# ScalarE takes the weights' low bits and batch 0's sums of squares, with a new order of work in the first stretch

## The chip, the cores and the metric

The kernel runs on one core of a Trainium2 chip. The metric is the device time of one execution in microseconds. The engines are TensorE (PE in the profile), VectorE (DVE), ScalarE (ACT), GpSimd (POOL) and SyncE (SP). SP, POOL and ACT also issue DMA transfers.

## The reference

Per batch (8) and head (8) there are 512 local and 32 global tokens of width 64. Global queries look at all keys; local queries look at the 32 global keys and at the local keys within 32 positions. The two outputs, in one tensor of 4608 x 512, go through a two-layer block: `h = x @ w_in` (512 x 2048), `g = h * tanh(log1p(exp(h)))`, `out = g @ w_out` (2048 x 512), in float32 at the end.

`w_in` and `w_out` come as float64, since a float32 array is scaled there by a float64 number. All else is float32. So the kernel sees each weight as two 32-bit words, and makes its float32 out of them with integer operations: bits 31 and 30 of the high word stay, its low 27 bits go up by three, and the top three bits of the low word come in below.

## The kernel before

**Tiling.** Attention goes by batch, pair of heads (hp, four of them) and query tile of 128 rows (t, four of them): scores (L895), row minimum with the mask (L921 on VectorE), exponential (L930 on ScalarE), a split of the result into two float16 parts, a transpose, and the product with V's two float16 parts (L1020). V's parts need a power of two as their scale, from the largest absolute value of the batch: `b_max` and `b_scale`, where POOL reduces over the partitions. For batch 0 the first two query tiles are transposed on TensorE (`p_cross`, L971 and L985; `x_cross`, L996 and L1004), which copies out of PSUM to `pt`, `xh` and `xl`.

The dense part goes by blocks of 256 tokens, 17 in all, and by eight slices of the inner dimension. The first product is `m1_mm` (L1173) and later `st_mm` (L1342); the second is `m2_mm` (L1437) and at the end `ms_mm` (L1532). Each float32 operand is again two float16 parts, three matmuls per product.

**Weights.** 32 blocks k of 128 x 512 float64 numbers, 0 to 15 of `w_in` and 16 to 31 of `w_out`, are loaded by `w_load` (512 KB each): 0 to 4 from ACT's queue, the others from POOL's. A load waits until its buffer is free. Per block VectorE runs `w_bits` (L630: shift and mask of the high word) and the two operations of `w_sum` (L637: the top two bits; L639: the low word, shifted). Then `w_stat` (L660) sums squares of the block on TensorE, and after the sixteenth block `w_norm` makes the scale from it: VectorE reduces (L671), POOL reduces over the partitions (L676), VectorE finishes. Only then `w_split` can write the float16 parts: the high ones on ScalarE (L537) or VectorE, the low ones on VectorE (L715), for the first four slices on TensorE (L709, L710) with a copy (L530). Loads 21 and up also wait for the reduction L671.

**Order.** [...] `Plan` gathers all tasks with their dependences, plays them against a table of costs and gives each engine a list. Then `MOVES` takes single tasks out of these lists: `231 P 196` puts task 231 right after task 196 on TensorE (P; V is VectorE, A ScalarE, G POOL, S the queue of SP). Tasks that may run on either engine change it in this way too. Each engine works through its list in order, and a waiting instruction holds up what is behind it.

Task numbers count the calls of `add`, so both versions number alike. Those that the prediction names:

- 196, 231: scores of batch 0, pair 0 and pair 1. 202, 211, 243: V's low parts of pairs 0 and 1, and the copy of pair 2's out of PSUM.
- 23: the identity times V's scale. 210, 250: V's high parts of pairs 1 and 3.
- 226, 288, 331: the copies of a `p_cross` out of PSUM (two instructions of 256 columns each); 304, 306, 337: those of an `x_cross` (one each).
- 342: a copy for `w_split` 1; 360, 382, 464: high parts of `w_split` 3, 4 and 7 (1024 columns). 402, 430, 479: high parts of probabilities. 462: an output of the global queries.
- 244, 253: the first small copy of V's rows for pairs 2 and 3, on SP's queue. 338: the load of batch 1's V, also there.

`VMAX` picks the batches whose V scale comes from squares on ScalarE; at 99 it picks none.

Of the kernel before, what the change touches and what calls it, by code (L numbers as in the profile page):

```python
# [73 lines left out]

MOVES = [(int(n), e, int(m)) for n, e, m in (x.split() for x in """91 P 271, 92 P 91, 93 P 92, 307 P 95, 284 P 275, 154 P 313, 350 P 154, 318 P 159, 164 P 330, 169 P 422, 174 P 343, 175 P 348, 176 P 358, 177 P 378, 178 P 392, 389 P 397, 398 P 389,
461 P 398, 179 P 421, 180 P 453, 454 P 180, 181 P 454, 450 P 474, 182 P 450, 475 P 182, 510 P 475, 183 P 510, 185 P 468, 557 P 555, 513 P 556, 526 P 558, 573 P 565, 566 P 573, 559
P 594, 664 P 642, 562 P 664, 580 P 562, 665 P 580, 680 P 665, 681 P 680, 703 P 622, 704 P 703, 625 P 629, 645 P 634, 666 P 645, 672 P 651, 652 P 672, 673 P 669, 705 P 673, 745 P
684, 747 P 745, 715 P 690, 716 P 708, 731 P 746, 732 P 748, 757 P 754, 769 P 757, 758 P 769, 818 P 783, 808 P 800, 35 V 18, 36 V 19, 37 V 20, 38 V 22, 232 V 39, 233 V 46, 43 V 233,
47 V 43, 44 V 47, 261 V 50, 262 V 54, 58 V 262, 56 V 62, 282 V 67, 283 V 71, 291 V 283, 296 V 291, 76 V 296, 267 V 81, 72 V 267, 73 V 83, 78 V 87, 292 V 88, 115 V 292, 111 V 115,
112 V 268, 274 V 297, 107 V 327, 101 V 107, 108 V 309, 103 V 322, 298 V 103, 104 V 298, 113 V 104, 380 V 113, 116 V 380, 328 V 116, 117 V 351, 123 V 119, 352 V 329, 127 V 366, 131  # L80
V 127, 373 V 424, 132 V 425, 133 V 135, 129 V 133, 374 V 129, 439 V 374, 381 V 136, 407 V 139, 137 V 407, 387 V 137, 403 V 387, 388 V 144, 370 V 388, 151 V 370, 371 V 151, 413 V
371, 372 V 413, 414 V 372, 418 V 414, 408 V 418, 384 V 408, 385 V 145, 148 V 448, 156 V 383, 157 V 431, 161 V 157, 412 V 161, 419 V 158, 449 V 419, 471 V 449, 149 V 471, 420 V 149,
396 V 466, 434 V 166, 459 V 401, 446 V 459, 163 V 171, 467 V 163, 168 V 172, 429 V 173, 472 V 429, 465 V 472, 529 V 465, 186 V 529, 480 V 186, 511 V 480, 534 V 188, 483 V 189, 457
V 483, 522 V 191, 512 V 478, 193 V 512, 524 V 193, 540 V 524, 535 V 540, 525 V 489, 195 V 525, 444 V 195, 906 V 444, 530 V 906, 536 V 531, 220 V 536, 907 V 220, 908 V 545, 230 V
908, 542 V 230, 260 V 550, 552 V 260, 520 V 560, 583 V 520, 584 V 583, 278 V 561, 910 V 578, 958 V 579, 587 V 585, 590 V 587, 591 V 588, 959 V 648, 649 V 959, 639 V 569, 620 V 639,
960 V 620, 961 V 960, 554 V 961, 786 V 554, 962 V 610, 624 V 962, 1001 V 643, 1002 V 644, 1003 V 1002, 575 V 1003, 1004 V 575, 687 V 1004, 1005 V 687, 1035 V 657, 621 V 1035, 1208
V 658, 688 V 1208, 1036 V 688, 667 V 678, 650 V 667, 631 V 650, 1037 V 631, 632 V 1037, 1209 V 632, 661 V 1209, 636 V 661, 668 V 636, 784 V 682, 637 V 683, 696 V 785, 697 V 810,
728 V 697, 729 V 706, 812 V 729, 654 V 707, 655 V 723, 700 V 655, 675 V 700, 813 V 1039, 676 V 813, 737 V 1062, 815 V 772, 738 V 815, 850 V 773, 1063 V 850, 730 V 1063, 693 V 1064,
694 V 752, 741 V 694, 718 V 741, 719 V 753, 1066 V 767, 768 V 1066, 776 V 1123, 821 V 776, 805 V 1124, 822 V 805, 806 V 1125, 779 V 734, 760 V 735, 761 V 790, 744 V 816, 1127 V
744, 1146 V 1127, 826 V 817, 1147 V 826, 823 V 1147, 787 V 823, 834 V 787, 797 V 834, 1148 V 797, 798 V 876, 802 V 798, 837 V 802, 803 V 864, 844 V 843, 235 A 226, 294 A 286, 295 A  # L90
294, 105 A 304, 317 A 105, 316 A 314, 312 A 316, 325 A 312, 335 A 331, 326 A 335, 355 A 340, 369 A 337, 342 A 438, 345 A 342, 440 A 344, 402 A 440, 360 A 347, 357 A 360, 359 A 349,
416 A 377, 379 A 416, 417 A 382, 451 A 417, 445 A 399, 395 A 445, 400 A 433, 462 A 400, 458 A 462, 427 A 458, 452 A 427, 469 A 452, 428 A 479, 463 A 428, 470 A 464, 477 A 456, 521
A 477, 482 A 521, 518 A 190, 192 A 443, 538 A 192, 539 A 538, 514 A 194, 219 A 514, 515 A 219, 527 A 515, 541 A 544, 528 A 229, 570 A 528, 519 A 259, 551 A 519, 277 A 551, 909 A
563, 279 A 564, 581 A 279, 567 A 582, 568 A 567, 711 A 609, 646 A 626, 656 A 627, 677 A 647, 713 A 677, 630 A 713, 635 A 630, 1038 A 660, 695 A 685, 720 A 686, 849 A 762, 692 A
849, 717 A 692, 740 A 717, 775 A 770, 804 A 771, 733 A 804, 836 A 833, 481 S 436, 523 S 485, 543 S 547, 640 S 593, 712 S 640, 659 S 749, 679 S 659, 714 S 679, 739 S 702, 764 S 739,
807 S 777""".split(","))]
# [1862 lines left out]
```

## Time and profile before

| | |
|---|---|
| median of 3 runs | 873.93 us (872.58 to 873.93) |
| the profiled execution | 873.65 us, of which the span is 871.9 |
| mean granted TensorE clock | 0.995 |
| DMA | 111.07 MB, mean 127 GB/s |

The span reaches from the first to the last instruction; 1.75 us of the execution lie around it. The page gives busy times over the whole span. The stages differ much, so the table of windows is the one to read first: each of its lines gives a stretch, its length, each engine's busy time in it with the number of instructions, the granted clock as a share of full speed, the mean busy share of the DMA engines, and GB/s. A busy engine is not always at its peak: the ends of matmuls are modelled.

### The profile page before, as it was taken

To read this page: it belongs to the slowest core of one execution; us is meant where nothing else is said; L and a number is where in the kernel's file an instruction comes from. 1 tells how busy PE (TensorE), PEld (TensorE's weight loads), DVE (VectorE), ACT (ScalarE), POOL (GpSimd) and SP (SyncE) were. 2 spreads that over 40 slices of the span, in tenths; PEclk is the share of its full clock that TensorE was granted. 3 is DMA by queue.
4 is the path that set the end of the run, shared out by engine and by line. 5 is a ranking of instruction groups with operands and counts; after the bars stand their busy time and mean duration, and the time that the engine had idled before them with its cause. 6 is when DMAs were issued, how large, how long until landed. Compare 5 with 4: busy or idle time off the path is not lost.

```text
span 871.9 us, 24740 instructions
## 1 busy us (share of the span) xinstructions
PE 840.7 (96%) x9792; PEld 620.8 (71%) x9792; DVE 747.9 (86%) x1989; ACT 645.9 (74%) x1389; POOL 169.4 (19%) x324
## 2 busy tenths in 40 slices
...
GB/s 365 372 358 92 120 153 115 60 145 101 180 216 124 194 136 131 150 107 183 126 121 104 170 131 101 89 165 121 122 116 118 89 77 38 1 27 14 14 27 25
DMA packets 206885, 111.07 MB, mean 127 GB/s; under 512 B 186992, under 2 KB 191280, under 8 KB 205744
## 3 DMA queue, kind: packets, MB, share of 16 engines
...
q10 hardware_dynamic: 864, 2.88, 0.9%
...
## 4 chain that ended last, share of the span: by engine, by line
PE 89%; DVE 6%; DMA 2%; ACT 1%; issue 0%; POOL 0%; DVEq 0%; ACTq 0%
PE o L1437 33%; PE h L1342 25%; PE h L1173 11%; PE s L895 5%; PE U L1020 5%; PE o L1532 5%; PE gu L1124 1%; PE g L1058 1%; DVE W L637 1%; DMA raw<-in_w 1%; DVE W L639 1%; DVE W L630 1%; DMA W<-in_w 1%; DMA pt<-ph 1%; PE hx L1532 1%; DVE vmx L744 1%
## 5 line engine op out<-in xcount | busy, mean ns | idle before, releaser
L1437 PE MATMUL o<-W,G 128*128 128x512 f16 x1344 | 313.2, 379 | 0.0
L1437 PEld LDWEIGHTS <-G 128*128 128x128 f16 x1344 | 124.9, 98 | 128.5 <-issue 2.6
L1342 PEld LDWEIGHTS <-W 128*128 128x128 f16 x2880 | 166.0, 98 | 9.6 <-issue 0.2
L930 ACT ACTIVATE P<-P,nm 128x192 f32<-128x192 f32 (+1 forms) x256 | 117.8, 461 | 38.8 <-DVE nm L921 38.2
L1173 PE MATMUL h<-xh,W 128*128 128x256 f16 x640 | 114.4, 273 | 0.0
L1173 PEld LDWEIGHTS <-W 128*128 128x128 f16 x960 | 91.1, 98 | 16.7 <-issue 3.0
L1342 PE MATMUL h<-xh,W 128*128 128x128 f16 x1056 | 97.0, 219 | 0.0
L1342 PE MATMUL h<-xl,W 128*128 128x128 f16 x528 | 91.1, 219 | 0.0
L1173 PE MATMUL h<-xl,W 128*128 128x256 f16 x320 | 87.2, 272 | 0.0
L1342 PE MATMUL h<-raw,W 128*128 128x128 f16 x1152 | 73.2, 219 | 0.0
L854 POOL DMA_DIRECT2D vc<-vf x81 | 41.3, 512 | 155.6 <-DVE vf L835 110.3
L1020 PEld LDWEIGHTS <-pt 128*128 128x128 f16 (+1 forms) x1424 | 56.1, 98 | 18.9 <-issue 7.7
L895 PE MATMUL s<-qk 64*128 64x224 f16 (+3 forms) x640 | 56.2, 301 | 7.3 <-DMA qk<-in_qk 6.4
L921 DVE CUSTOM_DVE_ANT_0 P<-s,consts,sq 128x192 f32<-128x192 f32 (+1 forms) x128 | 53.0, 429 | 10.3 <-PE s L895 10.3
L537 ACT ACTIVATE ph<-P 128x384 f16<-128x384 f32 (+1 forms) x112 | 58.7, 538 | 3.3 <-DMA pt<-ph 2.6
L854 POOL DMA_DIRECT2D vgg<-vgf x84 | 44.3, 531 | 85.0 <-issue 47.9
L921 DVE CUSTOM_DVE_ANT_0 P<-s,consts 128x192 f32<-128x192 f32 (+1 forms) x128 | 45.5, 369 | 9.0 <-PE s L895 4.4
L1020 PE MATMUL U<-vc,pt 96*128 96x64 f16 (+1 forms) x656 | 52.3, 193 | 0.0
L1020 PE MATMUL U<-vf,pt 128*128 128x64 f16 x720 | 50.7, 194 | 0.7 <-DMA pt<-ph 0.7
L930 ACT ACTIVATION_READ_ACCUMULATOR P<-P,nm 128x1 f32 x256 | 48.1, 188 | 0.0
L530 ACT COPY EE<-h 128x512 f32<-128x512 f32 x47 | 27.2, 579 | 23.4 <-PE h L1342 16.2
L949 DVE SCALAR_TENSOR_TENSOR ph<-P,ph 128x256 f16<-128x256 f32 x112 | 38.5, 353 | 4.1 <-ACT ph L537 3.5
(281 smaller groups left out, 1750.8 us busy)
## 6 DMA issues: line engine op xcount, KB each, us to landing
...
W<-in_w POOLq DMA_DIRECT2D x14, 512.0 KB, 7.5
raw<-in_w POOLq DMA_DIRECT2D x7, 512.0 KB, 7.3
G<-in_w POOLq DMA_DIRECT2D x6, 512.0 KB, 6.8
W<-in_w ACTq DMA_DIRECT2D x5, 512.0 KB, 10.6
pt<-ph SPq DMA_TRANSPOSE x120, 3.6
```

Of the source, the lines that this page charges most:

```text
L530: A.copy(dst, src)
L537: A.activation(out=dst, in_=src, func=AF.Copy, scale=c)
L854: stream(POOL, dma(kib), lambda: G.dma_start(dst(), src()), 512, r=[r], w=[w], new=new, table="dma")
L895: T.matmul(X[s[h]][:, cols(u)], part(b, hp, i)[r, u * 128:(u + 1) * 128], part(b, hp, j)[r, KO + OWN[u]:KO + OWN[u] + WIDTH[u]], start=n = ...
L921: pl.add(DVE, (134 if b >= QF else 77) + 1.03 * w, lambda: V.tensor_tensor_reduce(out=half(P, h, w), in0=X[s][:, cols(t)], in1=mask[:, m0: ...
L930: pl.add(ACT, 460, lambda: A.activation(out=half(P, h, w), in_=half(P, h, w), func=AF.Exp, bias=X[nm], scale=-1.0, accum_out=X[sums][:, t, ...
L949: pl.add(DVE, dve(2 * (z - a)), lambda a=a, z=z, q=q, o=o: V.scalar_tensor_tensor(X[ph][:, q, :, a + o:z + o], p_src(X[P], t)[:, :, a:z], ...
L1020: T.matmul(X[u][:, t, h, :], X[pt][:k, p * 4 + (c * 2 + h if turned(b, t) else h * 2 + c), :], X[vx][:k, t, vl, h * 64:(h + 1) * 64], star ...
L1173: T.matmul(X[h][:, f * TB:(f + 1) * TB], wh(i, wl)[:, off:off + 128], X[x][:, d, o:o + TB], start=(n == 0), stop=(n == 11))
L1342: T.matmul(X[h][:, c:c + 128], form(J + jj, wl)[:, off:off + 128], x(l, d), start=(p in (1, 2, 5) and c == 0 and n == 0), stop=(n == 5), s ...
L1437: T.matmul(X[o], gp(g, blk, i)[:, f, t * 128:(t + 1) * 128], wh(8 + i, wl)[:, f * 512:(f + 1) * 512], start=(turn == 0 and n == 0), stop=( ...
L1532: T.matmul(X[o][:, cols], a_form(a, jj, f), b_form(w, jj, f), start=(fresh and n == 0), stop=(n == 11), skip_group_check=True)
```

## The change

For each weight block, the second operation of `w_sum` on VectorE becomes a task of ScalarE: `w_low` reads the upper 16 bits of the low word, and by scale, bias and rounding to bfloat16 leaves their top three bits as the low bits of a bfloat16 number, which it writes over the lower half of the high word. The remaining VectorE operation, `w_join`, takes the top two and the low three bits of that word in one. `w_low` comes after `w_bits`, which still reads the whole high word, and `w_join` after `w_low`.

For batch 0 the V scale comes from the largest sum of squares of a partition, over 512 numbers (128 for the global rows), on ScalarE, instead of the largest absolute value on VectorE. `MOVES` is another list, of 413 entries instead of 344: 75 for TensorE (60 before), 213 for VectorE (199), 101 for ScalarE (74), 21 for SP (11) and 3 for POOL (none). Its highest task number stays the same. The diff is cut in the two lists; of the new one, the lines stand here that hold the entries named above.

```diff
@@ -14,6 +14,7 @@
 I32 = mybir.dt.int32
 U32 = mybir.dt.uint32
 BF16 = mybir.dt.bfloat16
+U16 = mybir.dt.uint16
 AF = mybir.ActivationFunctionType
 ALU = mybir.AluOpType
 AX = mybir.AxisListType
@@ -66,34 +67,39 @@
 STACKED = 1
 PELOW = 4
 STAT = 2
-VMAX = 99
+VSQ = (0,)
+BY_ACT = range(32)
 
 
 PE, DVE, ACT, POOL, DMA = "PE", "DVE", "ACT", "POOL", "DMA"
 
 
-MOVES = [(int(n), e, int(m)) for n, e, m in (x.split() for x in """91 P 271, 92 P 91, 93 P 92, 307 P 95, 284 P 275, 154 P 313, 350 P 154, 318 P 159, 164 P 330, 169 P 422, 174 P 343, 175 P 348, 176 P 358, 177 P 378, 178 P 392, 389 P 397, 398 P 389,
...
+MOVES = [(int(n), e, int(m)) for n, e, m in (x.split() for x in """231 P 196, 202 P 231, 211 P 202, 225 P 74, 237 P 225, 227 P 237, 242 P 84, 281 P 242, 239 P 281, 251 P 90, 269 P 91, 271 P 95, 234 P 97, 263 P 234, 100 P 287, 307 P 275, 284 P 299,
...
+745 P 684, 747 P 745, 715 P 690, 691 P 715, 716 P 708, 751 P 725, 746 P 751, 748 P 731, 818 P 783, 31 V 29, 35 V 31, 32 V 35, 20 V 198, 13 V 221, 37 V 13, 22 V 37, 34 V 22, 23 V
+34, 25 V 23, 38 V 222, 210 V 38, 232 V 210, 40 V 42, 46 V 40, 226 V 48, 50 V 261, 250 V 50, 266 V 262, 52 V 266, 243 V 54, 62 V 56, 283 V 58, 66 V 283, 71 V 60, 64 V 71, 68 V 292,
+78 V 68, 86 V 73, 296 V 86, 267 V 83, 297 V 267, 268 V 88, 274 V 107, 288 V 274, 308 V 109, 111 V 308, 327 V 309, 298 V 322, 104 V 115, 304 V 104, 328 V 119, 323 V 328, 351 V 323,
+306 V 351, 352 V 306, 121 V 352, 380 V 121, 405 V 123, 406 V 329, 331 V 406, 365 V 331, 384 V 125, 366 V 384, 423 V 127, 131 V 423, 424 V 131, 337 V 424, 425 V 337, 129 V 425, 370
+V 129, 135 V 370, 139 V 135, 371 V 139, 342 V 371, 439 V 342, 381 V 439, 373 V 381, 402 V 133, 374 V 402, 360 V 374, 387 V 360, 441 V 387, 388 V 441, 413 V 388, 137 V 413, 414 V
+137, 372 V 414, 403 V 372, 385 V 147, 382 V 156, 448 V 382, 383 V 448, 151 V 383, 407 V 166, 430 V 407, 149 V 431, 412 V 149, 419 V 412, 471 V 419, 396 V 471, 420 V 466, 459 V 420,
+171 V 459, 446 V 171, 434 V 446, 472 V 434, 408 V 168, 401 V 408, 464 V 401, 429 V 464, 529 V 429, 462 V 529, 465 V 173, 479 V 534, 480 V 535, 511 V 480, 457 V 511, 473 V 457, 512
...
+1147 V 826, 823 V 1147, 787 V 823, 834 V 787, 797 V 834, 1148 V 797, 798 V 876, 802 V 798, 837 V 802, 199 A 36, 200 A 199, 33 A 200, 223 A 201, 14 A 223, 224 A 39, 43 A 224, 47 A
...
+248, 338 S 253, 481 S 436, 596 S 481, 484 S 596, 485 S 484, 597 S 523, 750 S 597, 546 S 750, 547 S 546, 572 S 543, 592 S 589, 593 S 592, 712 S 640, 714 S 679, 662 S 714, 663 S 662,
...
@@ -634,6 +640,17 @@
         if not w64:
             return
         f, key = lambda: wf(k).bitcast(I32), wkeys(k)
+        if k in BY_ACT:
+
+            def w_low():
+                halves = raw(k).bitcast(U16).rearrange("p (f w) -> p f w", w=4)
+                A.activation(out=halves[:, :, 2].bitcast(BF16), in_=halves[:, :, 1], func=AF.Copy, scale=2.0 ** -8, bias=4336 + 2.0 ** -9)
+            pl.add(ACT, act(512), w_low, r=key, w=[rawkey(k)])
+
+            def w_join():
+                V.scalar_tensor_tensor(f(), word(k, 1), -0x3FFFFFF9, f(), ALU.bitwise_and, ALU.bitwise_or)
+            pl.add(DVE, 610, w_join, r=[rawkey(k)], w=key)
+            return
         pl.add(DVE, 610, lambda: V.scalar_tensor_tensor(f(), word(k, 1), -0x40000000, f(), ALU.bitwise_and, ALU.bitwise_or),
                r=[rawkey(k)], w=key)
         pl.add(DVE, 610, lambda: V.scalar_tensor_tensor(f(), word(k, 0), 29, f(), ALU.logical_shift_right, ALU.bitwise_or),
@@ -731,7 +748,7 @@
 
     def b_max(b, hp):
         m = ("vmx", b)
-        if b >= VMAX:
+        if b in VSQ:
             src = lambda: X["vraw", b][:, hp].rearrange("p a c -> p (a c)") if hp < HP else X["vgraw", b]
             n = 512 if hp < HP else 128
             pl.add(ACT, act(n) + 90, lambda: A.activation(out=junk[:, :n] if b > 1 else X["vj", b][:, :n], in_=src(), func=AF.Square, accum_out=X[m][:, hp:hp + 1]),
@@ -756,7 +773,7 @@
 
         def go():
             q, s = X[p], X[sv]
-            if b >= VMAX:
+            if b in VSQ:
                 V.tensor_scalar(q, q, TINY * TINY, None, ALU.max)
                 V.tensor_scalar(q.bitcast(I32), q.bitcast(I32), 1, 0x7F800000, ALU.logical_shift_right, ALU.bitwise_and)
                 V.tensor_scalar(q, q, 2.0 ** 63, None, ALU.mult)
@@ -1874,7 +1891,10 @@
         pl.settle()
 
     V.memset(pmax, 0.0)
-    pl.add(POOL, 600, lambda: G.partition_all_reduce(warm, pmax, 128, RED.max))
+
+    def warm_up():
+        G.partition_all_reduce(warm, pmax, 128, RED.max)
+    pl.add(POOL, 600, warm_up)
     for i, x in enumerate(ORDER.split()):
         a, n = x[0], int(x[1:] or 0)
         pl.slot = LOAD1 + LOADS1 * i
```

## Rows read from the trace of the kernel before

**Rows 1.** The page: busy time of each engine over the whole span.
```profile
PE 840.7 (96%) x9792; PEld 620.8 (71%) x9792; DVE 747.9 (86%) x1989; ACT 645.9 (74%) x1389; POOL 169.4 (19%) x324
```

**Rows 2.** The windows: one stage each; PE, PEld, DVE, ACT, POOL, clock, DMA.
```profile
0.00:6.37 6.37, 0.00 (x1) 0.00 (x1) 0.06 (x1) 1.28 (x1) 5.83 (x12) 1.00 0.71 243
6.37:20.00 13.63, 3.81 (x22) 2.48 (x24) 12.18 (x32) 2.45 (x9) 7.90 (x15) 1.00 1.03 416
20.00:45.00 25.00, 19.50 (x149) 13.14 (x148) 24.61 (x69) 13.52 (x41) 6.34 (x11) 0.86 1.02 371
45.00:70.70 25.70, 23.18 (x188) 14.19 (x188) 25.53 (x82) 23.04 (x67) 5.64 (x11) 1.00 0.92 320
70.70:110.00 39.30, 39.30 (x404) 30.03 (x402) 38.70 (x92) 36.54 (x66) 8.92 (x18) 1.00 0.42 100
110.00:145.00 35.00, 34.30 (x329) 24.18 (x328) 34.67 (x109) 30.25 (x63) 12.15 (x23) 1.00 0.73 141
200.00:800.00 600.00, 599.99 (x7399) 437.56 (x7396) 525.46 (x1409) 467.17 (x1014) 113.21 (x219) 1.00 0.61 116
800.00:872.00 72.00, 65.60 (x820) 60.70 (x817) 47.24 (x83) 30.71 (x51) 0.00 (x0) 0.99 0.08 24
```

**Rows 3.** The waits of PE, from 0 to 70.7 us, then to 800.
```profile
PE ws L660 <- DVE W L639: 13.2, 4, 6.7
PE s L895 <- DMA qk<-in_qk: 6.4, 1, 6.4
...
PE U L1020 <- DMA pt<-ph: 0.7, 1, 0.7
```

**Rows 4.** The timeline: last conversion, statistic, first split, first dense matmul.
```profile
40.28 1.28 DVE L639 SCALAR_TENSOR_TENSOR W<-W 128x512 int32<-128x512 int32 x2
44.99 0.28 DVE L671 CUSTOM_DVE_ANT_0 wd<-ws,consts 128x128 f32<-128x128 f32 x1
...
48.70 1.14 ACT L537 ACTIVATE W<-W,sw 128x1024 f16<-128x1024 f32 x1
...
70.69 0.27 PE L1173 MATMUL h<-xh,W 128*128 128x256 f16 x1
```

**Rows 5.** The sixteenth block's load: its issue on POOL, its time to landing.
```profile
31.35 0.53 POOL L612 DMA_DIRECT2D W<-in_w  x1 [2.43 <-DVE W L639]
...
W<-in_w POOLq DMA_DIRECT2D x1, 512.0 KB, 4.5
```

**Rows 6.** The chain of waits, from 12 to 20 us, on DVE.
```profile
14.32 1.78 DVE vmx L744 x3
16.10 0.34 DVE W L630
17.90 1.21 DVE W L639 x2
```

**Rows 7.** The groups by line: instructions of ACT that are nearest in kind.
```profile
L530 ACT CAST vf<-VT 128x512 f16<-128x512 f32 x3 | 1.8, 586 | 2.0 <-PE VT L831 2.0
L1088 ACT ACTIVATE gP<-g,gmx 128x512 f32<-128x512 f32 x8 | 5.4, 677 | 0.0
L537 ACT ACTIVATE W<-W,sw 128x1024 f16<-128x1024 f32 x16 | 18.3, 1144 | 1.9 <-DVE W L715 1.9
```

**Rows 8.** The waits of ACT to 70.7 us, of DVE to 145 us.
```profile
ACT t L537 <- DVE sv L547: 6.9, 1, 6.9
...
DVE p L764 <- POOL p L755: 0.3, 1, 0.3
```

**Rows 9.** The groups by line: instructions of DVE that are nearest in kind.
```profile
L539 DVE TENSOR_SCALAR G<-VX,c 128x1024 f16<-128x1024 f32 x24 | 18.0, 751 | 6.6 <-ACT VX L1371 6.6
...
L532 DVE CAST xh<-XT 128x256 f16<-128x256 f32 x1 | 0.4, 424 | 0.1
```

**Rows 10.** The windows: two stretches in which the clock fell.
```profile
35.00:40.00 5.00, 1.56 (x12) 1.04 (x13) 5.00 (x13) 0.80 (x4) 0.00 (x0) 0.72 1.03 375
40.00:45.00 5.00, 4.81 (x59) 4.34 (x58) 4.78 (x16) 1.17 (x5) 0.00 (x0) 0.60 1.02 334
```

More of the change, by code (lines that the diff above doesn't have):

```diff
@@ L77 @@
-P 594, 664 P 642, 562 P 664, 580 P 562, 665 P 580, 680 P 665, 681 P 680, 703 P 622, 704 P 703, 625 P 629, 645 P 634, 666 P 645, 672 P 651, 652 P 672, 673 P 669, 705 P 673, 745 P
-684, 747 P 745, 715 P 690, 716 P 708, 731 P 746, 732 P 748, 757 P 754, 769 P 757, 758 P 769, 818 P 783, 808 P 800, 35 V 18, 36 V 19, 37 V 20, 38 V 22, 232 V 39, 233 V 46, 43 V 233,
-47 V 43, 44 V 47, 261 V 50, 262 V 54, 58 V 262, 56 V 62, 282 V 67, 283 V 71, 291 V 283, 296 V 291, 76 V 296, 267 V 81, 72 V 267, 73 V 83, 78 V 87, 292 V 88, 115 V 292, 111 V 115,
@@ L80 @@
-112 V 268, 274 V 297, 107 V 327, 101 V 107, 108 V 309, 103 V 322, 298 V 103, 104 V 298, 113 V 104, 380 V 113, 116 V 380, 328 V 116, 117 V 351, 123 V 119, 352 V 329, 127 V 366, 131
-V 127, 373 V 424, 132 V 425, 133 V 135, 129 V 133, 374 V 129, 439 V 374, 381 V 136, 407 V 139, 137 V 407, 387 V 137, 403 V 387, 388 V 144, 370 V 388, 151 V 370, 371 V 151, 413 V
-371, 372 V 413, 414 V 372, 418 V 414, 408 V 418, 384 V 408, 385 V 145, 148 V 448, 156 V 383, 157 V 431, 161 V 157, 412 V 161, 419 V 158, 449 V 419, 471 V 449, 149 V 471, 420 V 149,
@@ L83 @@
-396 V 466, 434 V 166, 459 V 401, 446 V 459, 163 V 171, 467 V 163, 168 V 172, 429 V 173, 472 V 429, 465 V 472, 529 V 465, 186 V 529, 480 V 186, 511 V 480, 534 V 188, 483 V 189, 457
-V 483, 522 V 191, 512 V 478, 193 V 512, 524 V 193, 540 V 524, 535 V 540, 525 V 489, 195 V 525, 444 V 195, 906 V 444, 530 V 906, 536 V 531, 220 V 536, 907 V 220, 908 V 545, 230 V
-908, 542 V 230, 260 V 550, 552 V 260, 520 V 560, 583 V 520, 584 V 583, 278 V 561, 910 V 578, 958 V 579, 587 V 585, 590 V 587, 591 V 588, 959 V 648, 649 V 959, 639 V 569, 620 V 639,
@@ L86 @@
-960 V 620, 961 V 960, 554 V 961, 786 V 554, 962 V 610, 624 V 962, 1001 V 643, 1002 V 644, 1003 V 1002, 575 V 1003, 1004 V 575, 687 V 1004, 1005 V 687, 1035 V 657, 621 V 1035, 1208
-V 658, 688 V 1208, 1036 V 688, 667 V 678, 650 V 667, 631 V 650, 1037 V 631, 632 V 1037, 1209 V 632, 661 V 1209, 636 V 661, 668 V 636, 784 V 682, 637 V 683, 696 V 785, 697 V 810,
-728 V 697, 729 V 706, 812 V 729, 654 V 707, 655 V 723, 700 V 655, 675 V 700, 813 V 1039, 676 V 813, 737 V 1062, 815 V 772, 738 V 815, 850 V 773, 1063 V 850, 730 V 1063, 693 V 1064,
@@ L92 @@
-416 A 377, 379 A 416, 417 A 382, 451 A 417, 445 A 399, 395 A 445, 400 A 433, 462 A 400, 458 A 462, 427 A 458, 452 A 427, 469 A 452, 428 A 479, 463 A 428, 470 A 464, 477 A 456, 521
-A 477, 482 A 521, 518 A 190, 192 A 443, 538 A 192, 539 A 538, 514 A 194, 219 A 514, 515 A 219, 527 A 515, 541 A 544, 528 A 229, 570 A 528, 519 A 259, 551 A 519, 277 A 551, 909 A
-563, 279 A 564, 581 A 279, 567 A 582, 568 A 567, 711 A 609, 646 A 626, 656 A 627, 677 A 647, 713 A 677, 630 A 713, 635 A 630, 1038 A 660, 695 A 685, 720 A 686, 849 A 762, 692 A
@@ L95 @@
-849, 717 A 692, 740 A 717, 775 A 770, 804 A 771, 733 A 804, 836 A 833, 481 S 436, 523 S 485, 543 S 547, 640 S 593, 712 S 640, 659 S 749, 679 S 659, 714 S 679, 739 S 702, 764 S 739,
-807 S 777""".split(","))]
+MOVES = [(int(n), e, int(m)) for n, e, m in (x.split() for x in """231 P 196, 202 P 231, 211 P 202, 225 P 74, 237 P 225, 227 P 237, 242 P 84, 281 P 242, 239 P 281, 251 P 90, 269 P 91, 271 P 95, 234 P 97, 263 P 234, 100 P 287, 307 P 275, 284 P 299,
+154 P 303, 350 P 313, 159 P 315, 332 P 169, 422 P 386, 341 P 336, 343 P 341, 176 P 356, 177 P 378, 178 P 177, 397 P 392, 461 P 398, 389 P 461, 179 P 389, 421 P 179, 180 P 421, 181
@@ new lines @@
+P 415, 426 P 181, 474 P 453, 182 P 454, 450 P 182, 183 P 450, 510 P 183, 184 P 510, 185 P 468, 533 P 185, 475 P 533, 516 P 475, 532 P 516, 517 P 532, 537 P 517, 565 P 537, 566 P
+513, 526 P 566, 558 P 526, 577 P 556, 573 P 577, 562 P 664, 580 P 562, 574 P 681, 622 P 574, 703 P 622, 704 P 703, 625 P 629, 645 P 625, 666 P 645, 669 P 652, 705 P 673, 684 P 705,
+745 P 684, 747 P 745, 715 P 690, 691 P 715, 716 P 708, 751 P 725, 746 P 751, 748 P 731, 818 P 783, 31 V 29, 35 V 31, 32 V 35, 20 V 198, 13 V 221, 37 V 13, 22 V 37, 34 V 22, 23 V
@@ new lines @@
+V 188, 524 V 410, 483 V 524, 530 V 483, 478 V 191, 522 V 478, 906 V 522, 193 V 906, 540 V 193, 907 V 195, 531 V 907, 220 V 531, 545 V 220, 908 V 545, 230 V 536, 571 V 542, 500 V
+571, 260 V 550, 552 V 260, 520 V 560, 583 V 520, 584 V 583, 278 V 561, 910 V 578, 579 V 910, 958 V 579, 585 V 958, 590 V 587, 591 V 588, 959 V 648, 620 V 280, 569 V 620, 960 V 639,
+961 V 960, 554 V 961, 786 V 554, 962 V 610, 1001 V 643, 1002 V 644, 1003 V 1002, 575 V 1003, 1004 V 575, 687 V 1004, 1005 V 687, 1035 V 657, 621 V 1035, 1208 V 658, 688 V 1208,
@@ new lines @@
+1036 V 688, 678 V 1036, 650 V 667, 1209 V 650, 631 V 1209, 1037 V 631, 632 V 1037, 661 V 632, 636 V 661, 784 V 682, 637 V 683, 696 V 785, 728 V 810, 697 V 728, 721 V 811, 689 V
+721, 706 V 689, 729 V 706, 707 V 812, 654 V 707, 655 V 723, 700 V 655, 675 V 700, 1039 V 724, 676 V 813, 1062 V 676, 737 V 1062, 772 V 737, 738 V 815, 773 V 738, 763 V 773, 730 V
+1063, 752 V 693, 753 V 718, 1066 V 767, 1123 V 768, 776 V 1123, 1124 V 821, 805 V 1124, 1125 V 822, 734 V 774, 735 V 779, 761 V 790, 744 V 816, 1127 V 744, 1146 V 1127, 826 V 817,
```

11 lines of the change are left out of this document (7 added, 4 removed).

## The prediction

> **What bounds the kernel now.** I read the windows by stage first, because the whole-span shares hide the stages: TensorE is busy 96% of the span and looks like the bound everywhere [rows 1], yet from 70.7 to 800 us it has one wait of 0.7 us, and, but for 6.4 us at the end, all its idle time lies before 70.7 us [rows 2, 3]. There it is busy 0 + 3.81 + 19.50 + 23.18 = 46.5 us of 70.7 [rows 2]. So the time is, as a sum, when the dense matmuls of the first product begin (70.69 us [rows 4]), plus a stretch that TensorE fills, plus an end that the change does not touch. A microsecond is won only if that beginning comes earlier, and if the stretch behind it can follow.
>
> Next I asked what holds the beginning back. In the same windows VectorE is busy 24.61 of 25.00 us from 20 to 45, and 25.53 of 25.70 from 45 to 70.7; ScalarE only 2.45 of 13.63 and 13.52 of 25.00 before 45, but 23.04 of 25.70 after [rows 2]. The waits say the same: TensorE's largest is 13.2 us for the third conversion of a weight block (L639) [rows 3]. The weights' statistic needs all sixteen blocks of the first matrix, and VectorE finishes them at 40.28 + about 1.2 = 41.5 us; its last reduction starts at 44.99 and the first split weights come at 48.70 [rows 4]. The sixteenth load was issued at 31.35 us, held up by VectorE, and took 4.5 us to land: 35.9 [rows 5]. So 5.6 us lie between the data and the end of its conversion, and they are VectorE's backlog. But the DMA engines are no free resource: their share is 1.03 and 1.02 from 6.37 to 45 us [rows 2]. That is the second limit, just behind the first.
>
> **The change, part by part.** *Conversions.* Of three VectorE instructions for each of 32 blocks one goes away. Two of L639 in a row take 1.21 us on the chain, 0.605 each [rows 6]: 9.7 us for the first matrix, 9.7 for the second, 19.4 in all. ScalarE gets 32 copies of 512 elements; its nearest row is a cast of the same size, 0.586 us [rows 7], 18.8 us in all. Its two-byte operands lie eight bytes apart, which no row shows; I bound a copy by 0.4 (the cast shows no reason for less than two thirds) and 0.75 us (a scaled write of 1024 halves is 1.144 [rows 7]), and take 0.586.
>
> *V's scale.* Four reductions of 0.59 us leave VectorE (three take 1.78 [rows 6]): 2.4 us. ScalarE gets five squares; a 512-wide instruction with a running sum is 0.677 before its read-out [rows 7], so about 3.5 us, while it sat idle for 6.9 us up to exactly this scale [rows 8]. That idle time is the cover. If Square should need a table load I know no price but that of the loads already there; I take none, since plain copies show none. One more tiny VectorE operation in the scale is costed at nothing, beside the idle 0.3 us there [rows 8].
>
> *Tasks that change engine.* The new list names VectorE for five early ones that ScalarE did (23, 210, 226, 243, 250): two V halves at some 0.45, two 256-wide casts at 0.424, one 512-wide at 0.6, a small one at 0.25 [rows 9], 2.6 us. Of the first stretch VectorE thus loses 9.7 + 2.4 - 2.6 = 9.5 us. Behind 41 us it gets thirteen more: three weight splits (360, 382, 464) at 0.751, seven 256-wide casts at 0.424, the rest 2 us: 7.2 us against 9.7 removed, net -2.5. ScalarE gives away three splits of 1.144 and about 5 us more, 8.4, against 16 x 0.586 = 9.4 added [rows 7]: net +1.0. So the second half of the stretch is nearly level on both engines.
>
> *How much of the 9.5 us counts.* The code's loads up to the sixteenth block are 12.7 MB (four of 704 KB, 272 KB, 1088 KB, sixteen of 512 KB). By the measured rates, 243 GB/s to 6.37 us and 416 to 20, 7.2 MB have come by 20 us; the other 5.5 MB at 371 GB/s take 14.7 us [rows 2], so the block lands at 34.7 at best and at 35.9 at worst. Behind it stand one shift (0.34 on the chain [rows 6]), one copy, one join: 0.34 + 0.59 + 0.61 and two hand-overs, 2.0 us. The statistic's input is then done at 36.7 to 37.9 instead of 41.5: 3.6 to 4.8 us earlier, and I take 4.2. What remains of the 9.5 us turns into VectorE waiting for DMA.
>
> *The clock.* [...] At 0.60 about four fifths of 4.81 us ran at half speed, 1.9 us too long. Less waiting ahead of it should give some back: between 0 and 1.9, I take 0.6, since most of it lies beside VectorE's chain.
>
> *Orders.* On TensorE the second head pair's scores (231) and V's low halves (202, 211) go ahead of the first statistics; behind them those statistics queue, which nobody needs before 36 us. If the second q/k tile lands late, the wait is hidden by the 6 us that TensorE waited there anyway [rows 3]. On SyncE the last two pairs' first copies (244, 253) and batch 1's V load (338) are placed anew, one transfer of 1 MB among those that fill the DMA engines; the copies that move past it win what it loses. On POOL three copies of batch 1 swap, beyond 90 us. I cost these at nothing; bounds -1 to +1 us.
>
> Sum: -4.2 - 0.6 = -4.8, with -6.7 - 1 and -3.6 + 1 as bounds. The profiled run took 873.65 us (a span of 871.9 and 1.75 around it); the median, 873.93, stands 0.28 above. 873.65 - 4.8 + 0.28 = **869.1 us**.
>
> **Rivals.** *A, the forecast*: data-bound at 36.7 to 37.9 us, 866 to 871.5.
>
> *B, VectorE's whole saving counts*: loads come earlier too, because their buffers are freed earlier (POOL waited 2.43 us for one [rows 5]), and 9.5 us arrive: 864.4. Against it: the DMA share is full already.
>
> *C, the hand-overs eat it*: each block now goes VectorE, ScalarE, VectorE. VectorE hardly idled; a wait for another engine cost it 0.3 us [rows 8]. If each of the 16 early joins waits that long in order, 4.8 us are gone and the time is 873.9: no change.
>
> *D, ScalarE becomes the bound, slower*: from 45 to 110 us it idles only 2.66 + 2.76 = 5.4 us [rows 2]. Sixteen copies there need 9.4. Should the relief of 8.4 not arrive in time (the copies stand in front of the exponentials, the pt casts and the splits in one queue), TensorE waits for 9.4 - 5.4 = 4.0 us: 877.9. It decides once ScalarE's added work in this window passes 5.4 us. Against it: the list takes off about as much as it adds. [...]
>
> **Chances.** A 0.58, B 0.15, C 0.13, D 0.14. What a measurement of this kernel can tell from no change is about 0.2%, 1.75 us: faster means below 872.2. A and B are faster, and a small part of C: 0.75. The rest of C is 0.11. D is 0.14. The range goes down to 863.5 to take in B with its clock gain, and up to 874.5, past C; most of D stays out. A's own range is 866 to 871.5.
>
> **What would show it.** Right: L639 is gone and 32 ScalarE copies near 0.59 us are there; VectorE shows idle time until a DMA for W between 20 and 37 us; the last join ends near 37, the last statistic reduction starts near 41, the first L1173 near 66; the later gaps of TensorE stay under 1 us. The clock stays at its higher level longer in 35 to 45. Wrong: a copy of 0.8 us or more; VectorE idle behind the copies (C); TensorE idle behind ScalarE between 60 and 130 us (D); loads landing before 33 us (B).

## The result, and the profile after

The changed kernel takes **882.18 us** (882.15 to 882.24), the kernel before in the same runs 873.25 (872.32 to 873.93): a ratio of 1.0103, 95% interval 1.0086 to 1.0121. It is 8.9 us slower, where 869.1 and faster were forecast, and lies beyond the top of the range. Of the four cases it comes nearest to D, ScalarE as the bound, and is worse than D's 877.9.

The groups by line on ScalarE and the copy's partner on VectorE show the reason in one column. Columns: line, engine, operation, tile and shapes, count, then busy time and mean ns, then idle time before them and what ended it. `W`, `raw` and `G` are the buffers in which the weight blocks lie.

```profile
L647 ACT ACTIVATE W<-W 128x512 bf16<-128x512 uint16 x19 | 25.0, 1354 | 9.4 <-DVE W L636 8.8 <-ACT P L947 0.6
L647 ACT ACTIVATE raw<-raw 128x512 bf16<-128x512 uint16 x7 | 9.3, 1373 | 0.0
L647 ACT ACTIVATE G<-G 128x512 bf16<-128x512 uint16 x6 | 8.2, 1360 | 0.0
L754 ACT ACTIVATE vj<-vraw 128x512 f32<-128x512 f32 x4 | 2.4, 601 | 1.2 <-DMA vraw<-in_vm 1.1
...
L651 DVE SCALAR_TENSOR_TENSOR W<-W 128x512 int32<-128x512 int32 x19 | 13.1, 691 | 10.6 <-ACT W L647 10.5
```

The squares cost what was taken for them (0.60 us). The copies do not: 1.35 to 1.37 us each, 25.0 + 9.3 + 8.2 = 42.5 us in all against 18.8 in the forecast and beyond its upper bound of 0.75 us a copy. The windows by stage (the last one 8 us longer, as the span is 880.3) show where the 23.7 us more went:

```profile
6.37:20.00 13.63, 3.51 (x16) 2.29 (x16) 6.64 (x25) 10.00 (x21) 6.34 (x13) 1.00 1.03 416
20.00:45.00 25.00, 16.98 (x122) 11.25 (x122) 17.84 (x54) 22.65 (x43) 6.49 (x12) 0.81 1.00 354
45.00:70.70 25.70, 22.11 (x186) 13.70 (x187) 22.30 (x73) 24.89 (x60) 6.08 (x11) 0.99 0.79 303
70.70:110.00 39.30, 35.10 (x376) 27.83 (x375) 33.80 (x91) 37.25 (x61) 3.34 (x6) 1.00 0.47 96
110.00:145.00 35.00, 35.00 (x308) 22.69 (x305) 34.21 (x92) 31.32 (x67) 16.60 (x32) 1.00 0.70 149
200.00:800.00 600.00, 599.99 (x7368) 435.89 (x7367) 524.34 (x1422) 470.31 (x1026) 119.47 (x231) 1.00 0.62 118
800.00:880.00 80.00, 74.04 (x928) 68.63 (x925) 54.99 (x95) 34.40 (x56) 0.00 (x0) 0.99 0.07 21
```

Read the third and fourth numbers behind the length, VectorE and ScalarE, against [rows 2]. Before, VectorE was the full column from 20 to 70.7 us (24.61 and 25.53) and ScalarE had 11.5 us free from 20 to 45. Now ScalarE is nearly full (22.65 and 24.89), and VectorE has 7.2 + 3.4 us free. The bottleneck has changed sides. TensorE's column falls to 110 us by 0.30 + 2.52 + 1.07 + 4.20 = 8.1 us; from 110 us on it is as full as before. So the loss lies ahead of 110 us.

The waits say who holds whom, first those of VectorE, then of TensorE, both from 6 to 110 us (total, times, longest):

```profile
DVE W L651 <- ACT W L647: 10.5, 15, 1.4
DVE W L636 <- DMA W<-in_w: 8.2, 2, 6.1
DVE W L651 <- ACT raw L647: 2.5, 4, 1.0
DVE W L651 <- ACT G L647: 2.0, 2, 1.6
```

```profile
PE s L912 <- DMA qk<-in_qk: 16.3, 2, 9.5
PE PT L988 <- ACT P L947: 3.4, 1, 3.4
PE h L1190 <- ACT EE L1236: 3.4, 3, 2.1
```

VectorE waits 15.0 us, 21 times, for a copy. TensorE's 13.2 us for the conversion [rows 3] are gone, but they did not become work: the wait for the q/k tile grew from 6.4 to 16.3 us, since the second pair's scores now stand second in its queue, and two waits for ScalarE came on. (The long wait for q/k is no part of the loss: a run below has it as well, 16.1 us, and is fast.)

The timeline has the milestones of [rows 4]: the sixteenth block's join ends at 44.9 instead of 41.5 (it still waited 0.31 us for its copy), the statistic stands at 47.09 instead of 44.99, the first dense matmul at 75.82 instead of 70.69.

```profile
44.25 0.69 DVE L651 SCALAR_TENSOR_TENSOR W<-W 128x512 int32<-128x512 int32 x1 [0.31 <-ACT W L647]
...
47.09 0.28 DVE L688 CUSTOM_DVE_ANT_0 wd<-ws,consts 128x128 f32<-128x128 f32 x1
```

```profile
75.82 0.27 PE L1190 MATMUL h<-xh,W 128*128 128x256 f16 x1
```

Those 5.1 us, and the 3.4 us that the dense matmuls then wait for EE (ScalarE's activation of a first product) where they waited 0.7 before [rows 3], make 7.8 of the 8.4 us by which the span grew. The chain of waits, followed through the middle of the stretch, shows the queue that makes them: copies (L647) between exponentials (P), evictions (pt) and splits (W), each released by the one ahead of it.

```profile
53.32 1.04 ACT W L543
54.36 1.24 ACT raw L647
55.60 0.27 ACT P L947 x2
55.87 0.54 ACT pt L543 x2
56.41 0.90 ACT P L947 x4
57.30 0.47 ACT W L536
```

### The profile page after: what moved, and what is told of

Its sections match the earlier page's. It is cut to its first block, busy times and chain, and to the rows that moved or that the text cites. A ratio compares the mean times of both kernels' runs of the same rounds, so it can differ in the third digit from the quotient of the medians.

```text
span 880.3 us, 24756 instructions
## 1 busy us (share of the span) xinstructions
PE 841.7 (96%) x9792; PEld 620.8 (71%) x9792; DVE 735.7 (84%) x1974; ACT 673.7 (77%) x1410; POOL 168.9 (19%) x324
## 4 chain that ended last, share of the span: by engine, by line
PE 87%; ACT 6%; DVE 2%; issue 1%; DVEq 0%; ACTq 0%
PE o L1454 33%; PE h L1359 25%; PE h L1190 11%; PE s L912 5%; PE U L1037 5%; PE o L1549 5%; PE g L1075 1%; PE gu L1141 1%; ACT pt L543 1%; ACT W L647 1%; ACT raw L647 1%; ACT G L647 1%; ACT P L947 1%; PE hx L1549 1%; ACT W L543 1%
## 5 line engine op out<-in xcount | busy, mean ns | idle before, releaser
L912 PE MATMUL s<-qk 64*128 64x224 f16 (+3 forms) x640 | 55.4, 301 | 16.3 <-DMA qk<-in_qk 16.3
L536 ACT COPY EE<-h 128x512 f32<-128x512 f32 x47 | 27.2, 579 | 23.7 <-PE h L1359 16.7
```

The source lines that it names most:

```text
L536: A.copy(dst, src)
L912: T.matmul(X[s[h]][:, cols(u)], part(b, hp, i)[r, u * 128:(u + 1) * 128], part(b, hp, j)[r, KO + OWN[u]:KO + OWN[u] + WIDTH[u]], start=n = ...
```

## The experiments

In the diffs the kernel is the one after unless said otherwise. Theory 1: the copy's operand form costs 1.36 us, so ScalarE is the bound. Theory 2: the new order costs the time. (Where an expectation says 1.24 us, it is a copy's length on the chain of waits above; as an instruction it is 1.36.)

**The copy's form, four ways.** Each changes one line of the copy. In the first, with both sides in a row:

```
-   A.activation(out=halves[:, :, 2].bitcast(BF16), in_=halves[:, :, 1], func=AF.Copy, scale=2.0 ** -8, bias=4336 + 2.0 ** -9)
+   A.activation(out=raw(k).bitcast(U16)[:, 512:1024].bitcast(BF16), in_=raw(k).bitcast(U16)[:, 0:512],
+                func=AF.Copy, scale=2.5 / 65536, bias=-1.25)
```

> Leaves out the move of the low bits: each of the 32 ScalarE copies reads the first 512 halfwords of its block in a row and writes 512 bf16 in a row over other words of the block (so a quarter of the weights becomes other random numbers); plan, order, joins and squares are those of the kernel after. If the operand's form makes the copy cost 1.24 us (theory 1): a copy falls to about 0.59 us mean, ScalarE's busy time falls by 32 x 0.65 = 21 us, VectorE's waits for the copies from 15.0 us to under 5, and the run comes to 867 to 872 us. If the new order of the scores or the hand-overs are to blame (theory 2): the copy may fall but the run stays at 879 to 883 us. If 2-byte sources cost this much in any form, the copy stays at 1.24 us and the time stays too.

Then only the read in a row (the source is halfwords 1536 to 2047), only the write in a row (the destination is halfwords 0 to 511), and the read of a whole 32-bit word:

> Leaves out the right low bits: the copy reads 512 halfwords in a row, and writes them, as the kernel after does, to every fourth halfword. If the write at an 8-byte step is the dear side, the copy stays at 1.3 to 1.4 us and the time at 880 to 883 us; if the read is, the copy falls to about 0.6 us and the time to 867 to 872 us; if both sides share it, the copy lies between (0.9 to 1.1 us), and the time near 875 us.

> Leaves out the place of the low bits: the copy reads every fourth halfword, as the kernel after does, and writes 512 bf16 in a row over the block's first words (a quarter of the weights becomes other random numbers). The mirror of the copy that reads in a row: if the write is the dear side 0.6 us a copy and 867 to 872 us, if the read is 1.3 to 1.4 us and 880 to 883 us, if both share it 0.9 to 1.1 us and near 875 us.

> Same computation as the kernel after, but the copy reads the whole low word (32 bits, at a step of 8 bytes) instead of its upper halfword, with scale 2^-24 for 2^-8. If reading two bytes out of eight is what costs, as against reading four, the copy falls to about 0.6 us and the time to 867 to 872 us; if the write costs, or the step of 8 bytes whatever the width, nothing changes: 1.3 to 1.4 us a copy, 880 to 883 us.

Measured, as ratios to the kernel before: plain 869.5 us, 0.9941 [0.9925, 0.9958]; read in a row 881.9, 1.0085 [1.0070, 1.0100]; write in a row 870.5, 0.9952 [0.9935, 0.9970]; whole word 881.8, 1.0085 [1.0070, 1.0100]. The copies' rows in the groups by line, in this order:

```profile
L647 ACT ACTIVATE W<-W 128x512 bf16<-128x512 uint16 x19 | 11.7, 625 | 11.0 <-DVE W L636 10.1 <-DVE rs L1045 0.4 <-ACT P L947 0.3
```
```profile
L647 ACT ACTIVATE W<-W 128x512 bf16<-128x512 uint16 x19 | 25.1, 1362 | 9.3 <-DVE W L636 8.8 <-ACT P L947 0.6
```
```profile
L647 ACT ACTIVATE W<-W 128x512 bf16<-128x512 uint16 x19 | 12.4, 665 | 11.3 <-DVE W L636 10.7 <-ACT P L947 0.3
```
```profile
L647 ACT ACTIVATE W<-W 128x512 bf16<-128x512 uint32 x19 | 25.0, 1356 | 9.4 <-DVE W L636 8.8 <-ACT P L947 0.6
```

The write alone makes the price: 0.625 and 0.665 us with it in a row, 1.36 without, whatever the read. What VectorE waits for these copies falls with it, from 15.0 to 2.0 us (waits of VectorE with plain copies, 6 to 145 us):

```profile
DVE W L651 <- ACT W L647: 2.0, 3, 0.7
```

And the price alone turns the sign: with cheap copies in the same plan and the same order, the time is 869.5 (868.68 to 869.97), where 869.1 was forecast. So the new order alone does not make the loss of the kernel after. With plain copies the windows of the same stages are nearly full on TensorE again:

```profile
20.00:45.00 25.00, 19.32 (x171) 13.08 (x171) 20.20 (x65) 17.91 (x51) 8.22 (x16) 0.93 1.04 377
45.00:70.70 25.70, 24.45 (x205) 15.55 (x204) 24.92 (x77) 24.69 (x68) 3.57 (x7) 1.00 0.97 314
70.70:110.00 39.30, 38.94 (x382) 28.25 (x380) 38.05 (x96) 36.85 (x68) 7.02 (x14) 1.00 0.55 111
```

Its timeline, first on VectorE (the sixteenth block's join and the statistic), then on TensorE (the first dense matmul):

```profile
37.52 0.69 DVE L651 SCALAR_TENSOR_TENSOR W<-W 128x512 int32<-128x512 int32 x1
...
42.05 0.28 DVE L688 CUSTOM_DVE_ANT_0 wd<-ws,consts 128x128 f32<-128x128 f32 x1
```
```profile
67.42 0.27 PE L1190 MATMUL h<-xh,W 128*128 128x256 f16 x1
```

The join ends at 38.2 us, and the dense matmuls begin 3.3 us ahead of [rows 4]. What lies between the join and the statistic is no longer the weights. The chain of waits, followed back from there, goes through a small transfer of V's rows (`vc`), which the product with V (U) needs; the last sums for the statistic stand behind that product in TensorE's list:

```profile
31.06 7.67 DMA vc<-vgf
38.86 0.44 PE U L1037 x9
39.33 0.44 DVE x L1047
```

TensorE waits 1.8 us for that transfer and VectorE 1.1 us for U. No run moves it, so what it would be worth is not shown.

**What in the write costs.** One kernel with seven forms of the write, one for every seventh block. `u` is the block as halfwords and `z` as fp32; the forms are, from block 0 to block 6: bf16 at a step of 4 bytes, fp32 at 8 bytes, fp32 in a row, bf16 pairs at 8 bytes, bf16 at 8 bytes, 256 bf16 at 16 bytes, bf16 in a row.

```
+   out = [u[:, 0:1024].bitcast(BF16).rearrange("p (f w) -> p f w", w=2)[:, :, 0],
+          z.rearrange("p (f w) -> p f w", w=2)[:, :, 0],
+          z[:, :512],
+          u[:, 0:1024].bitcast(BF16).rearrange("p (f w) -> p f w", w=4)[:, :, 0:2],
+          u.bitcast(BF16).rearrange("p (f w) -> p f w", w=4)[:, :, 0],
+          u.bitcast(BF16).rearrange("p (f w) -> p f w", w=8)[:, :, 2],
+          u[:, :512].bitcast(BF16)][k % 7]
+   A.activation(out=out, in_=src, func=AF.Copy, scale=2.5 / 65536, bias=-1.25)
```

> The kernel after with the copy's write in seven forms, one for every seventh block (leaves out the low bits; some weights become other random numbers): 512 bf16 in a row, 512 bf16 at a step of 4 bytes, 512 bf16 at a step of 8 bytes on another halfword, 256 bf16 at a step of 16 bytes, 512 bf16 as pairs at a step of 8 bytes, 512 fp32 at a step of 8 bytes, 512 fp32 in a row. Known ends: 0.63 us in a row, 1.36 us at 8 bytes. If it is the narrow write (under 4 bytes apart from its neighbour) that costs, fp32 at 8 bytes and the pairs take 0.6 to 0.7 us and bf16 at a step of 4 bytes takes 1.3 to 1.4 us. If it is the step of 8 bytes, fp32 at 8 bytes takes 1.3 to 1.4 us, and bf16 at 4 bytes lies between or at 0.65 us. The time means nothing here: 868 to 878 us.

The first seven on ScalarE's timeline (start, duration) are blocks 0, 1, 3, 2, 4, 5 and 6:

```profile
7.65 0.78 ACT L660 ACTIVATE W<-W 128x512 bf16<-128x512 uint16 x1 [5.64 <-DVE W L636]
8.63 0.67 ACT L660 ACTIVATE W<-W 128x512 f32<-128x512 uint16 x1 [0.20 <-DMA W<-in_w]
15.56 0.65 ACT L660 ACTIVATE W<-W 128x512 bf16<-128x512 uint16 x1
16.99 0.64 ACT L660 ACTIVATE W<-W 128x512 f32<-128x512 uint16 x1
19.34 1.33 ACT L660 ACTIVATE W<-W 128x512 bf16<-128x512 uint16 x1
20.85 1.33 ACT L660 ACTIVATE W<-W 128x256 bf16<-128x256 uint16 x1
22.50 0.66 ACT L660 ACTIVATE W<-W 128x512 bf16<-128x512 uint16 x1
```

Neither guess holds whole. The step of 8 bytes alone is free (fp32 and bf16 pairs: 0.67 and 0.65 us), and the single halfword alone is nearly so (0.78 at a step of 4 bytes). Single halfwords at a step of 8 bytes cost double, and 256 of them at 16 bytes as much as 512 at 8, so about double again for each (there the read's step is 16 bytes too; that was not taken apart). The kernel ran once, 872.0 us; only its instructions are read here.

**The order, apart from the conversion.** An order here is the whole list of moves, with the engines that it names. Two runs put ScalarE's copy and the new join into the kernel before, at the places of its two merges in VectorE's list; no place was sought for the copy among ScalarE's other work:

```
-   pl.add(DVE, 610, lambda: V.scalar_tensor_tensor(f(), word(k, 1), -0x40000000, ...),
+   pl.add(DVE, 610, w_low,
...
-   pl.add(DVE, 610, lambda: V.scalar_tensor_tensor(f(), word(k, 0), 29, f(), ALU.logical_shift_right, ALU.bitwise_or),
+   pl.add(DVE, 610, lambda: V.scalar_tensor_tensor(f(), word(k, 1), -0x3FFFFFF9, f(), ALU.bitwise_and, ALU.bitwise_or),
```

> The kernel before with its own compute orders and no squares on ScalarE: only the conversion is exchanged, the ScalarE copy standing where the first merge stood and the new join where the second did. If the dear copy is the cause (theory 1), 32 copies of 1.36 us fill ScalarE here too, and the run is slower than before by 3 to 10 us: 877 to 884 us. If the new order of the scores is to blame (theory 2), the old order does better than the new one: 868 to 874 us.

> As the one before it, but the copy reads 512 halfwords in a row and writes 512 bf16 in a row over other words of the block (leaves out the low bits and puts other random numbers in a quarter of the weights), at about 0.63 us each. If the new order brings nothing by itself, this comes to 867 to 871 us, like the kernel after with plain copies (869.5). If the gain of that one came from its order, this stays at 872 to 876 us.

And two do the reverse: the new order with VectorE's merges (`vector_all`: `w_join` gets the first and `w_low` the second of the two lines removed above), and the kernel before with the squares alone.

> The kernel after with its orders and its squares, but each copy and join is done by VectorE with the two merges of the kernel before, at the places of the copy and the join. ScalarE is free of 43 us, VectorE carries 32 x 0.6 = 19 us more than in the kernel after. If the order is neutral (theory 1): 872 to 876 us, the time of before. If the new order costs time by itself (theory 2): 878 us or more. If the order was laid for conversions off VectorE, VectorE's queue may be late at places where the lists do not expect it: 876 to 880 us.

> The kernel before with batch 0's value magnitudes taken by ScalarE as sums of squares (four instructions of 0.60 us and one small one) at the places of the VectorE maxima, all else as before. VectorE is free of 4 x 0.59 us while it waits for loads anyway: 872.5 to 874.5 us, no change; if batch 0's value scale holds up the first stretch, up to 1.5 us faster.

Measured: old order with dear copies 896.4 us, 1.0237 [1.0220, 1.0253]; with plain copies 879.6, 1.0044 [1.0029, 1.0059]; new order with VectorE's merges 882.4, 1.0075 [1.0054, 1.0096]; squares alone 874.6, 0.9989 [0.9980, 0.9999] (the kernel before took 875.9 in these runs). The two with the old order lie outside all that was expected, and VectorE's merges in the new order came out where theory 2 had put them: I had held order and conversion for separable, and they are not. A cheap copy loses 0.4% in the old order and wins 0.6% in the new; the new order with the old conversion loses 0.75%. So of these pairs each order does best with the conversion it was laid for. Each pair is one placement; that no other place for the copy in the old order would pay is not shown. In the old one with dear copies VectorE, whose queue expects two merges in a row, stands behind the copies (waits of VectorE):

```profile
DVE W L645 <- ACT W L641: 21.2, 14, 3.8
```

**What VectorE's time is worth.** First the low bits are left out altogether: in the kernel after (`w_low` does nothing and the join sets the top bits alone) and in the kernel before (without its second merge). The first is called `no_low` further on.

> The kernel after without the copies; the join sets the top bits alone, so the three lowest of the 24 bits of each weight are left out. What remains of the change: VectorE with two instructions a block, nothing added to ScalarE but the squares, the new orders. If the plain copies of 0.63 us still held something up (hand-overs, rival of the prediction), this is faster than the 869.5 us of that run: 864 to 868 us. If they were hidden: 868.5 to 870 us.

> The kernel before without its second merge, so the three lowest of the 24 bits of each weight are left out: VectorE is rid of 32 x 0.60 us, ScalarE gets nothing, the orders are those of before. If what VectorE is rid of is worth its whole time between 45 and 110 us (the prediction's rival of 864.4): 862 to 866 us. If the data of the first 45 us bound it, as the prediction says: 866 to 871 us. If the old order cannot use the time: 871 to 874 us.

The new order gives 868.8 us, 0.9942 [0.9925, 0.9959], the same as with plain copies: 32 cheap copies and their hand-overs are hidden entirely. The old order gives 872.7, 0.9984 [0.9975, 0.9994]: VectorE is rid of 16.9 us (747.9 to 731.0 busy), and 1.4 us arrive. Its timeline of VectorE shows why:

```profile
36.91 0.69 DVE L637 SCALAR_TENSOR_TENSOR W<-W 128x512 int32<-128x512 int32 x1
37.52 0.39 DVE L921 CUSTOM_DVE_ANT_0 P<-s,consts 128x224 f32<-128x224 f32 x1
...
41.60 0.43 DVE L630 TENSOR_SCALAR W<-raw 128x512 int32<-128x512 int32 x1 [3.68 <-DMA raw<-in_w]
...
44.81 0.28 DVE L671 CUSTOM_DVE_ANT_0 wd<-ws,consts 128x128 f32<-128x128 f32 x1
```

The last merge of the first matrix ends at 37.6, where the forecast put it. But the old order then has the shift of a block of the second matrix, which is still on its way: VectorE stands 3.68 us, and the statistic's reduction (L671) queues behind it, though TensorE has summed the last block by 40.7. The statistic comes at 44.81 instead of 44.99. In the new order that queue is laid otherwise, and with the low bits left out it comes at 41.25.

Next, VectorE's time is put back into the kernel after with plain copies: the join is done twice. (`low_first`, which the expectation names, is the first of the versions below that keep the values.)

> The kernel after with plain copies (which leaves out the low bits and puts other random numbers in a quarter of the weights) and each join done twice in a row by VectorE: 32 x 0.65 us of VectorE's time put back at the join's own place, nothing else. If low_first kept its 881.6 us for its two merges at the join's place: 879 to 883 us here. If VectorE's time there has room: 869.5 to 873 us, and low_first's loss came from something else (writing int32, or the copy that now waits for the load alone).

It takes 888.6 us, 1.0159 [1.0144, 1.0175]: 19.1 us more for the 20.6 us that VectorE's busy time grew (735.5 to 756.1). The dense matmuls begin at 78.42, and TensorE's wait for the conversion, 13.2 us in [rows 3] and 0.5 with plain copies, is back in part (waits of TensorE; the second join is its L652):

```profile
PE ws L678 <- DVE W L652: 6.3, 3, 2.4
```

So in this order VectorE's time counts over nine tenths, once ScalarE is out of the way.

**Versions that keep the values.** Since a write of whole words is cheap (0.64 us in a row, 0.67 at a step of 8 bytes), ScalarE can put the three bits as int32 into the block's own place (`low` is the low words, at a step of 8 bytes), and VectorE merges twice:

```
+   A.activation(out=f(), in_=low, func=AF.Copy, scale=2.0 ** -29, bias=2.0 ** -20 - 0.5)
...
+   V.scalar_tensor_tensor(f(), word(k, 1), 3, f(), ALU.logical_shift_left, ALU.bitwise_or)
+   V.scalar_tensor_tensor(f(), word(k, 1), 0x3FFFFFFF, f(), ALU.bitwise_or, ALU.bitwise_and)
```

> Same values as the kernel after but for a rounding of the last bit in rare cases: ScalarE writes the three low bits as 512 int32 in a row into the block's own place (from the low words, at a step of 8 bytes), and VectorE then merges in two two-input instructions, at the place of the join. A copy takes about 0.65 us, VectorE's three-bit shift of 0.34 us becomes a merge of 0.65 us: 32 x 0.3 = 10 us more on VectorE than with plain copies, but no way back from VectorE to ScalarE. If write form was all that was wrong with the change: 869 to 874 us, at or under before. If VectorE's extra 10 us all stand in the way between 45 and 110 us: 874 to 877 us. If writing int32 is dear as well: over 878 us.

The next two (`low_early` and a variant) move the copy and the first merge ahead, to the place of the shift; the last splits the dear copies between the engines (`if k % 2` the merges of `vector_all`, else the copy).

> The instructions of low_first, differently placed: ScalarE's copy of the low bits about 1.2 us ahead of the place of the three-bit shift, the first merge at the place of the shift, only the second at the place of the join. VectorE's sum is that of low_first, 10 us above plain copies. If place is what counts (VectorE waits for data where the shift stands and has the time there): 870 to 875 us. If the sum counts: 879 to 882 us. If ScalarE's copies, now ahead of others, hold ScalarE's other work up: 875 to 879 us.

> As low_early, with the copies up to 3 us ahead (never ahead of their load): fewer waits of VectorE for a copy, more waits of ScalarE's other work. Within 2 us of low_early either way: 870 to 877 us.

> The kernel after with the dear copy for every other block, the rest merged by VectorE as in vector_all, at the same places: ScalarE carries 16 x 1.36 = 22 us instead of 43, VectorE 16 x 0.6 = 10 us more than after. Both ends stood at 882. If the loss is a sum that one engine is made to carry (ScalarE in one, VectorE in the other), the middle lies under both: 872 to 878 us. If the new order itself costs, it stays at 880 to 883 us.

Measured: 881.6 us, 1.0086 [1.0071, 1.0101]; placed early 877.9, 1.0038 [1.0025, 1.0051] and 877.2, 1.0033 [1.0022, 1.0044]; half and half 876.0, 1.0017 [1.0008, 1.0027]. The cheap write is there (groups by line of the first), but the merge that replaces a shift costs VectorE 0.3 us a block more (0.69 us, where the shift took 0.42 to 0.43):

```profile
L647 ACT ACTIVATE W<-W 128x512 int32<-128x512 uint32 x19 | 12.4, 668 | 9.0 <-DMA W<-in_w 6.1 <-DVE W L652 2.9
```

So its 881.6 lies over 878, but not because writing int32 is dear, as that branch of the expectation had it. Its 12.1 us above plain copies exceed the 9.2 us that VectorE carries more (744.7 against 735.5 busy); at the shift's place a third of the 12.1 comes back, so part of it was the place of the first merge. The first placement falls into its third branch (875 to 879), the second just past its 877; VectorE now waits at the shift for the copy instead of the load (16.2 us, and 16.5 with the copies up to 3 us ahead). The middle of ScalarE and VectorE lies under both ends, as expected of a sum that one engine has to carry, but not under the kernel before. With all 24 bits of the weights kept, none but the squares alone (0.1%) came out under it. The one that beats both kernels by more is `no_low`: 868.8 us, at the price of the three lowest of the 24 bits of each weight.

## Why the prediction was wrong

The step that failed is in "Conversions": "its nearest row is a cast of the same size, 0.586 us ...; I bound a copy by 0.4 ... and 0.75 us". The copy measured 1.36 us. The text named the reason for doubt ("Its two-byte operands lie eight bytes apart, which no row shows") and still set the upper bound by a row with a write in a row. The copy came to 2.3 times the cast's row. Even a bound of twice that row, 1.17 us, would have been short, but it would have shown the danger: sixteen copies are then 18.8 us, which less the relief of 8.4 pass rival D's threshold of 5.4. The sign of being wrong that the text names first, a copy of 0.8 us or more, is the one that came.

- *ScalarE's load.* Rival D reckons 16 copies less the 5.4 us idle [rows 2], with the relief of 8.4 not arriving. With 1.36 us that is 21.8 - 5.4 = 16.4, 890.3 us; with the relief taken off as well, 8.0, 881.9 us. Measured 882.2. So the rival had the engine and the threshold, and the same mis-sized term, but the agreement of the second sum is partly luck. D puts all of the loss between 45 and 110 us; of the 8.1 us that TensorE lost to 110 us, 2.8 lie before 45, where the other sixteen copies already made the last join 3.4 us late.
- *V's scale.* Right: 0.60 us a square, hidden; the squares alone are worth 0.1%.
- *The data bound.* Near, once the price is right: with plain copies the sixteenth load, issued at 30.07, lands after 6.2 us at 36.3 (34.7 to 35.9 said), the last join ends at 38.2 (36.7 to 37.9), the statistic stands at 42.05 (41), the dense matmuls begin at 67.42 (66), and the time is 869.5 (869.1). Each milestone is later than said, and the statistic waits behind V's transfer, which the prediction does not have. That the time still comes within 0.4 us is in part luck.
- *Rival C, the hand-overs.* Wrong: without any copy the time is the same as with plain ones. What VectorE waits in the kernel after, 15.0 us, comes from the copy's length, not the hand-over: with plain copies it is 2.0.
- *Rival B, the whole saving of VectorE.* Not reached in either order: 16.9 us less on VectorE gave 1.4 us in the old order, and in the new one it ends at 868.8, where VectorE waits 11.3 us for loads (waits of VectorE without copies, 6 to 145 us):

```profile
DVE W L636 <- DMA W<-in_w: 11.3, 6, 5.6
```

Put back into the run with plain copies, VectorE's time counts almost whole (19.1 of 20.6 us). Up to the last join the bound is the data, and VectorE stands right behind it.
- *Orders.* "I cost these at nothing" was wrong in its form, though not in its sum. The order decides whether a gain can pass: with plain copies the new one is 1.0% better (0.9941 against 1.0044), with VectorE's merges and the squares 0.9% worse (1.0075 against 0.9989). With plain copies the time came out as forecast only in the order that suits the new conversion; that it would matter the prediction had not examined, so here it was lucky.
- *The clock.* From 35 to 40 and 40 to 45 us the granted clock was 0.72 and 0.60 [rows 10]; in windows of 1 us it stood at 0.50 to 0.51 from 38 to 44 us, and at 1.00 just before 37 and from 44 on. After, it is lower:

```profile
35.00:40.00 5.00, 2.61 (x19) 2.37 (x20) 3.05 (x9) 5.00 (x9) 1.24 (x3) 0.55 0.98 343
40.00:45.00 5.00, 3.75 (x42) 3.14 (x41) 3.64 (x10) 5.00 (x13) 0.00 (x0) 0.50 1.06 358
```

TensorE does 6.36 us of work in these ten, at a granted clock of 0.55 and 0.50. With plain copies the two stretches have 0.98 and 0.67, so there the term had the right sign; its 0.6 us was the author's estimate, and no run shows it apart from the rest.
